# Seven half products for eight in part of layer 1, with conversions in parts and later maxima

## The chip, the cores and the metric

The kernel runs on one core of a Trainium2 chip. TensorE multiplies matrices from SBUF into the accumulator memory PSUM; VectorE, ScalarE and GpSimd work elementwise; the SyncE queue issues most of the transfers. The metric is the device time of one execution in microseconds (us), as the median over runs.

## The reference

Three stages follow one another. Attention gives 1792 tokens of 768 features. Layer 1 makes the largest of three products, and layer 2 projects it. A routed expert layer with two further products ends the program. Layer 1, where the change lies, is this:

```python
def _moe_ref(x, w1, w2, w3, w_out):
    h = np.maximum(np.maximum(x @ w1, x @ w2), x @ w3)   # 1792 x 768, weights 768 x 768
    return (h @ w_out).astype(np.float32)
```

The weights come as 64-bit floats. The kernel turns them into 32-bit ones with integer operations on the two halves of each number.

## The kernel before, in words

Every product is made with 32-bit operands split in two, a rounded part R and the rest L, as three matmuls: R by R, R by L, L by R. In layer 1 the weight is the stationary operand, 128 rows of a feature block at a time, and the tokens stream past it. The 1792 tokens lie as a piece of 1024 and a piece of 768, and the 768 output features are six blocks. `project` (L489) makes one piece of one block of one weight: 6 contraction blocks by 3 matmuls by 2 halves, so 36 matmuls of 512 columns for the piece of 1024, and 36 of 384 columns for the piece of 768. The loop at L529 to L532 goes over block, piece and weight. The first weight of a piece is copied out of PSUM by ScalarE (L503); the second and third are joined by VectorE as a maximum with what lies in SBUF (L505). The result `hT` stays in SBUF: four blocks in `hA` and two in `hB`. PSUM gives these products two buffers in turn (`ps_a`, L160), so a piece must be evacuated before the piece after next begins.

TensorE, ScalarE, VectorE and SyncE run in the order in which the program is written (`manual_schedule`); each is a strict queue, and semaphores make an instruction wait for the others. Layer 1's weights are 18 chunks of 768 x 256 words; w_out gives another 6 of the same size. SyncE loads them into two `stage` buffers (`load_chunk`, L217). VectorE converts one in six operations (`cv_ops`, L166), then ScalarE rounds it and VectorE takes the rest (`split`, L183, with the engines' lines L188 and L189) into one of four slots of `w_ring`. This work and the 48 products that fold the gate matrix into w_out (`gate_op`, L479) lie in two lists, `bg` and `bg2`. `background` (L243) takes operations off them behind each piece until a budget of estimated time is spent. The first four chunks are converted during attention, whose last evacuations are L370 and L371 (`evac_X`).

At the end of layer 1 `split_a` and `split_h` split the first operands of layer 2, which reads the tokens in tiles of 128 (`pass_a`, L566). The expert layer already has products of 384 columns in a scheme with seven products in place of eight (`mm2_prod`, L919); its matmuls have the line L928.

## Time and profile before

| | us |
|---|---|
| median of 3 runs (735.32 to 735.49) | 735.34 |
| the profiled execution itself | 731.45 |
| its span | 729.6 |
| TensorE busy in the span | 721.0 (99%) |
| VectorE busy | 486.5 (67%) |
| ScalarE busy | 263.2 (36%) |
| GpSimd busy | 77.0 (11%) |

The span covers the instructions, and 1.85 us of the profiled execution lie around it. A busy time is the time in which the engine had at least one instruction in work. Matmuls overlap one another in the records, so one matmul's own duration is longer than its share of the stream. The chain of waits is followed back from the last instruction, and its shares say what the span consists of.

### The profile page before, as it was taken

Reading aid. Unit: us, or ns where it says so; the run is one execution under the profiler, and the core shown is the slowest. Engines: PE = TensorE matmul, PEld = TensorE weight load, DVE = VectorE, ACT = ScalarE, POOL = GpSimd, SP = SyncE. Lnnn points to the kernel's source line nnn. Section 1 sums busy time; section 2 is a strip of 40 time slices with the busy share of each in tenths; the row PEclk is TensorE's granted clock in tenths of the full one; section 3 lists DMA queues with packets and bytes.
Section 4 is the critical chain, followed back from the end, with each engine's and each line's share of the span. In section 5 each row is a group of like instructions: output and inputs, shape, how many; then the busy total and the mean of one; then the engine's idle time right before and its main releaser. Section 6 shows DMA issues by size and latency. Waiting matters only on the chain.

```text
span 729.6 us, 10665 instructions
## 1 busy us (share of the span) xinstructions
PE 721.0 (99%) x4164; PEld 613.9 (84%) x4164; DVE 486.5 (67%) x845; ACT 263.2 (36%) x410; POOL 77.0 (11%) x96
## 2 busy tenths in 40 slices
PE   8999999999999999999999999999999999999996
PEld 5455545799898988989899988998998899999996
DVE  4677885666877879873125657146895698689363
ACT  5665566000011010100123533243661474375352
POOL 3000000000000000000001004453025005101101
PEclk9999999999999999999999999999999999999999
DMA  8856761141332321310000113668154025515101
GB/s 204 214 158 167 195 185 54 44 130 54 124 129 91 95 94 44 108 44 1 0 1 22 66 53 126 191 190 308 57 190 158 0 75 174 199 53 193 51 2 63
DMA packets 42330, 78.58 MB, mean 108 GB/s; under 512 B 6201, under 2 KB 28794, under 8 KB 42276
## 3 DMA queue, kind: packets, MB, share of 16 engines
q1 hardware_dynamic: 38420, 66.10, 30.0%
q0 software_dynamic: 3776, 11.63, 4.6%
q8 instruction: 35, 0.57, 0.3%
q14 instruction: 19, 0.16, 0.1%
q10 hardware_dynamic: 80, 0.11, 0.1%
HBM read 69.79 MB, written 11.58 MB: 112 GB/s over the span
## 4 chain that ended last, share of the span: by engine, by line
PE 98%; DMA 0%; SPq 0%; issue 0%; DVE 0%; POOL 0%; POOLq 0%; ACT 0%; ACTq 0%
PE acc L499 36%; PE hacc L900 16%; PE oacc L928 12%; PE X L344 8%; PE s L318 7%; PE acc_b L563 5%; PE acc_a L563 4%; PE oacc L916 3%; PE acc_c L563 3%; PE X L352 2%; PE xT L788 1%; PE s L334 1%; DMA u<-in_qk_dram 0%; SPq L269 0%; PE wgp L360 0%
## 5 line engine op out<-in xcount | busy, mean ns | idle before, releaser
L499 PE MATMUL acc<-xR,w_ring 128*128 128x512 f32 (+1 forms) x864 | 208.3, 362 | 0.0
L499 PEld LDWEIGHTS acc<-xR,w_ring 128*128 128x128 f32 x864 | 157.6, 188 | 17.6 <-issue 0.7
L900 PE MATMUL hacc<-xh,wo_ck 128*128 128x512 f32 (+3 forms) x600 | 120.6, 361 | 0.0
L900 PEld LDWEIGHTS hacc<-xh,wo_ck 128*128 128x128 f32 x600 | 107.1, 188 | 12.1 <-DVE xo L948 0.3
L499 PE MATMUL acc<-xLa,w_ring 128*128 128x512 f32 (+1 forms) x360 | 101.3, 362 | 0.0
L301 ACT ACTIVATE at<-s,nlns 128x896 f32<-128x896 f32 x84 | 77.9, 1007 | 44.4 <-PE s L318 43.0
L928 PE MATMUL oacc<-wo_ck,hx 128*128 128x384 f32 x504 | 90.3, 336 | 0.0
L928 PEld LDWEIGHTS oacc<-wo_ck,hx 128*128 128x128 f32 x504 | 87.2, 188 | 0.2
L189 DVE TENSOR_TENSOR wo_ck<-raw,wo_ck 128x512 fp32r<-128x512 f32 (+1 forms) x87 | 68.4, 807 | 24.6 <-ACT wo_ck L188 24.5
L499 PEld LDWEIGHTS acc<-xLa,w_ring 128*128 128x128 f32 x360 | 66.3, 188 | 7.1
L188 ACT ACTIVATE wo_ck<-raw 128x512 fp32r<-128x512 f32 (+1 forms) x87 | 59.6, 723 | 18.6 <-DVE raw L823 7.6
L318 PEld LDWEIGHTS s<-kq 64*128 64x128 f32 x432 | 37.9, 185 | 21.3 <-issue 15.5
L318 PE MATMUL s<-kq 64*128 64x448 f32 x432 | 50.9, 376 | 0.8 <-ACT kq L287 0.8
L503 ACT ACTIVATE hA<-acc 128x1024 f32<-128x1024 f32 (+1 forms) x8 | 7.4, 922 | 118.3 <-PE acc L499 118.3
L480 DVE SCALAR_TENSOR_TENSOR gk<-wof,gk 128x768 f32<-128x768 f32 x48 | 45.9, 957 | 1.4
L997 POOL MEMSET xo<- 128x544 f32 x5 | 2.6, 550 | 410.6 <-PE acc_a L563 382.1
L775 POOL DMA_INDIRECT xg<-x2d,idx x30 | 36.5, 1218 | 74.1 <-PE xT L788 43.8
L344 PE MATMUL X<-at,u 128*64 128x448 f32 x192 | 37.8, 543 | 0.0
L370 DVE CAST xR<-X 128x448 fp32r<-128x448 f32 x24 | 14.9, 619 | 31.9 <-PE X L352 31.9
L505 DVE TENSOR_TENSOR hB<-hB,acc 128x1024 f32<-128x1024 f32 (+1 forms) x8 | 8.7, 1088 | 39.5 <-PE acc L499 39.4
L188 ACT ACTIVATE w_ring<-cv 128x768 fp32r<-128x768 f32 x14 | 11.8, 842 | 54.7 <-PE acc L499 54.7
L505 DVE TENSOR_TENSOR hA<-hA,acc 128x1024 f32<-128x1024 f32 (+1 forms) x16 | 17.4, 1087 | 20.3 <-PE acc L499 19.9
(260 smaller groups left out, 885.2 us busy)
## 6 DMA issues: line engine op xcount, KB each, us to landing
stage<-in_moe_w_dram SPq DMA_DIRECT2D x18, 768.0 KB, 4.5
raw<-in_moe_w_dram SPq DMA_DIRECT2D x12, 1024.0 KB, 5.7
u<-in_qk_dram SPq DMA_DIRECT2D x46, 224.0 KB, 4.8
raw<-in_moe_w_dram SPq DMA_DIRECT2D x12, 768.0 KB, 4.8
stage<-in_moe_w_out_dram SPq DMA_DIRECT2D x6, 768.0 KB
x2d<-xo SPq DMA_DIRECT2D x28, 128.0 KB, 1.7
gk<-wgT SPq DMA_DIRECT2D x8, 384.0 KB, 5.4
rawb<-in_moe_w_dram SPq DMA_DIRECT2D x4, 768.0 KB, 4.6
```

The lines of the kernel that those rows point to most:

```text
L188: nc.scalar.activation(out=r(dR), in_=src, func=ACTF.Copy)
L189: nc.vector.tensor_tensor(out=r(dL), in0=src, in1=dR, op=ALU.subtract)
L301: nc.scalar.activation(out=dst, in_=s[:, :, 0:S], func=ACTF.Sigmoid, scale=qscale, bias=nlns)
L318: nc.tensor.matmul(s[g][:, h, 0:S], r(kt[p, a, 0, 128 * g:128 * (g + 1)]), r(kt[p, x, 1]), start=(n == 0), stop=(n == 2))
L344: nc.tensor.matmul(X_t[u][64 * h:64 * h + 64, 0:S], vt[:, 2 * g + h], at[:, 2 * g + h], start=(g == 0), stop=False)
L480: nc.vector.scalar_tensor_tensor(out=junk, in0=wof[kb], scalar=1.0, in1=wgb[e % 2], op0=ALU.mult, op1=ALU.mult, accum_out=gw[:, kb, e:e + 1])
L499: nc.tensor.matmul(acc[:, c, 0:cw], r(m[:, a, kk, :]), r(x[kk][:, c0 + cw * c:c0 + cw * (c + 1)]), start=(kk == 0 and n == 0), stop=(kk == ...
L505: nc.vector.tensor_tensor(out=dst, in0=dst, in1=acc[:, :, 0:cw], op=ALU.max)
L563: nc.tensor.matmul(acc, r(hs[:, a, kk, :]), r(w(kk, b)), start=(kk == 0 and n == 0), stop=(kk == KB - 1 and n == 2))
L775: d = nc.gpsimd.indirect_dma_start(out=xg[s][:, XC[c][0]:XC[c][1]], out_offset=None, in_=x2d[c], in_offset=bass.IndirectOffsetOnAxis(ap=ix ...
L900: st["mm"] = nc.tensor.matmul(acc[:, f, t0:t1], r(w[a][:, k, 128 * f:128 * (f + 1)]), r(x[:, 2 * c + k, t0:t1]), start=(t0 == 0 and c == 0 ...
L928: nc.tensor.matmul(o[:, s, 0:HC], r(hz[k][:, x, 2 * c + f, 128 * s:128 * (s + 1)]), r(w[a][:, f]), start=(first and c == 0 and f == 0 and ...
```

## The change

Layer 1's work becomes nine jobs: a pair of feature blocks (256 features) with one of the three weights. Jobs 0 to 4 are made as before, except that the piece of 768 tokens comes first and the order is pair, weight, piece. In jobs 5 to 8 the piece of 768 tokens is made by the Winograd form of Strassen's scheme: the weight pair is a 2 x 2 arrangement of quarters (two feature blocks by two halves of the contraction), the tokens another (two halves of the contraction by two times 384 tokens), and seven half products of 9 matmuls of 384 columns take the place of eight (`s_block`). For that the token operands T1, T2 and T4 are summed and split during job 0 (`t_prep`), T3 in job 4 in the place of an operand that is no longer needed (`t3_prep`), and for each job four sums of weight quarters are made (`s_sums`) and split (`s_split`). The products go to three PSUM banks, two of which are read between two accumulations; VectorE adds the parts and takes the maximum.

A conversion is now one ScalarE copy with a scale and four VectorE operations, and its parts are written between the reads of the products (`hook`). From chunk 16 on there is one stage buffer, and the next load is issued when a conversion has ended. In jobs 5 to 8 the maxima of the piece of 1024 come one piece later (`held`). T4, T1 and T2 lie where `hA` was, so the blocks of the first two pairs are written to DRAM (`spill`) and read back into `hA` in four loads in the last job. The tokens are numbered anew in layer 2 (`tok`), with the piece of 768 first. At the end of attention one further chunk is loaded, and two conversions are begun.

```diff
+    def conv_start(load=True):
+        k = nk[0]
+        nk[0] += 1
+        if k < NC1 and load:
+            load_chunk()
+        v = cv1 if k >= NC1 or k % 2 == 0 else cv2
+        st = stage[k % 2 if k < NC1 else 0]
+        hf = st.bitcast(F32).rearrange("p (n two) -> p n two", two=2)[:, :, 1]
+        nc.scalar.activation(out=v, in_=hf, func=ACTF.Copy, scale=E64_SC)
+        return k, v, st
...
+    def conv_mid(c):
+        v = c[1]
+        ve = nc.vector
+        ve.tensor_scalar(out=v, in0=v, scalar1=-E64_TOP, scalar2=E64_TOP, op0=ALU.max, op1=ALU.min)
+        ve.tensor_scalar(out=v.bitcast(I32), in0=v.bitcast(I32), scalar1=3, scalar2=None, op0=ALU.logical_shift_left)
+    def conv_fin(c, dsts):
+        k, v, st = c
+        st = st.rearrange("p (n two) -> p n two", two=2)
+        lo, hi = st[:, :, 0], st[:, :, 1]
+        ve = nc.vector
+        ve.scalar_tensor_tensor(out=v.bitcast(U32), in0=lo.bitcast(U32), scalar=29, in1=v.bitcast(U32),
+                                op0=ALU.logical_shift_right, op1=ALU.bitwise_or)
+        for d, c0, c1 in dsts or [(v, 0, DM)]:
+            ve.scalar_tensor_tensor(out=d.bitcast(U32), in0=hi[:, c0:c1].bitcast(U32), scalar=0x80000000,
+                                    in1=v[:, c0:c1].bitcast(U32), op0=ALU.bitwise_and, op1=ALU.bitwise_or)
+        if k >= NC1:
+            load_chunk()
...
+    NJOB, FJ = 3 * (KB // 2), 5
...
+    chunks = [wch(j, f) for j in range(2) for f in range(2)] + och(0, 1, 2, 3, 4)
+    chunks += [wch(2, 0)] + och(5) + [wch(2, 1)] + [wch(j, f) for j in range(3, FJ) for f in range(2)]
+    NC1 = len(chunks)
+    assert NC1 % 2 == 0
+    chunks += [wch(j, f) for j in range(FJ, NJOB) for f in range(2)]
+    ring_no = {wch(j, f)[1:]: 2 * (j % 2) + f for j in range(FJ) for f in range(2)}
...
-                background(2.5, stop=(1, 0))
+                background(2.5, stop=(1, 1))
+            if j == NU // 2 - 1:
+                background(99, stop=(1, 1))
+                load_chunk()
             emit_av(A)
             emit_av(B)
-        background(99, stop=(1, 0))
+            if j == NU // 2 - 1:
+                c0 = conv_start(False)
+                early = [c0, conv_start(False)]
+                for c in early:
+                    conv_mid(c)
...
+        SW = (NT - HALF) // 2
+        K2 = KB // 2
+        NQ = K2 * SW
+        S0_, S1_ = slice(HALF, HALF + SW), slice(HALF + SW, NT)
+        tT = hold("H1", "tT", 3, 2, K2, SW)
...
+        def t_prep():
+            tt = hold("K1", "tt", 2, K2, SW)
+            tA, tB = tt[:, 0], tt[:, 1]
+            whole = lambda a: [(slice(0, K2), a)]
+            ops = minus_plus(tA, (xpart(0, 0, S1_)[0][1], xpart(0, 0, S0_)), [(SUB, xpart(1, 0, S0_)), (ADD, xpart(1, 0, S1_))])
+            ops.append(lambda: split(tT[:, 0, 0], tT[:, 0, 1], tA))
+            ops += minus_plus(tB, (xpart(0, 1, S1_)[0][1], whole(tA)), [(ADD, xpart(1, 1, S1_))])
+            ops.append(lambda: split(tT[:, 1, 0], tT[:, 1, 1], tB))
+            ops += minus_plus(tA, (xpart(0, 1, S0_)[0][1], whole(tB)), [(ADD, xpart(1, 1, S0_))])
+            ops.append(lambda: split(tT[:, 2, 0], tT[:, 2, 1], tA))
+            return ops
...
+        def t3_prep():
+            t = cut(sm_[0], 0, K2, SW)
+            for op in minus_plus(t, (xpart(0, 1, S1_)[0][1], xpart(0, 0, S1_)), [(SUB, xpart(1, 0, S1_)), (ADD, xpart(1, 1, S1_))]):
+                op()
+            split(xR_[:, 0:K2, S1_], xLa[:, 0:K2, S1_], t)
...
+        raw_a = [cut(us[i], 2 * DM, QW) for i in range(2)]
+        raw_b = [cut(cv2, QW * i, QW) for i in range(2)]
+        DST = ([(raw_a[i], QW * i, QW * (i + 1)) for i in range(2)], [(cv2, 0, 2 * QW)])
+        def part(i):
+            return cut(sm_[0], QW * i, QW)
+        def s_sums():
+            ve_ = nc.vector.tensor_tensor
+            ve_(out=part(0), in0=raw_b[0], in1=raw_b[1], op=ALU.add)
+            ve_(out=part(1), in0=part(0), in1=raw_a[0], op=ALU.subtract)
+            ve_(out=part(2), in0=raw_a[0], in1=raw_b[0], op=ALU.subtract)
+            ve_(out=part(3), in0=raw_a[1], in1=part(1), op=ALU.subtract)
...
+        def s_split(i):
+            m = sw_[i]
+            split(flat(m[:, 0]), flat(m[:, 1]), cut(sm_[0], 2 * QW * i, 2 * QW))
+        def split_aw(f):
+            if f:
+                split(flat(aw[1][:, 0]), flat(aw[1][:, 1]), cv2)
+                return
+            for k, src in enumerate(raw_a):
+                split(ksl(aw[0], 0, k), ksl(aw[0], 1, k), src)
...
+        def prod(a, b, g, first):
+            a, b = aop(a), bop(b)
+            for kk in range(K2):
+                for n, (i, x) in enumerate(((0, 0), (0, 1), (1, 0))):
+                    nc.tensor.matmul(g[:, 0:SW], r(a(i, kk)), r(b(x, kk)), start=(first and kk == 0 and n == 0),
+                                     stop=(kk == K2 - 1 and n == 2), skip_group_check=not first)
...
+        def s_block(hp, wi, hook):
+            g0, g1 = (ps(f"x{i}", [128, 512], f"g{i}") for i in range(2))
+            g2 = ps("t", [128, 2, 512], "g2")[:, 0]
+            t1, t2, t3, t4 = (part(i) for i in range(4))
+            c = slice(0, SW)
+            ve_ = nc.vector.tensor_tensor
+            def fin(u, g, dst):
+                d = dst if wi == 0 else t4
+                ve_(out=d, in0=u, in1=g[:, c], op=ALU.add)
+                if wi:
+                    ve_(out=dst, in0=dst, in1=t4, op=ALU.max)
+            prod("A11", "B11", g0, True)
+            nc.scalar.activation(out=t1, in_=g0[:, c], func=ACTF.Copy)
+            hook(0)
+            prod("S2", "T2", g1, True)
+            ve_(out=t2, in0=t1, in1=g1[:, c], op=ALU.add)
+            hook(1)
+            prod("A12", "B21", g0, False)
+            take(g0[:, c], hp[:, 0, S0_], wi)
+            hook(2)
+            prod("S1", "T1", g2, True)
+            hook(3)
+            prod("S3", "T3", g1, False)
+            ve_(out=t3, in0=t1, in1=g1[:, c], op=ALU.add)
+            fin(t3, g2, hp[:, 1, S1_])
+            hook(4)
+            g3 = ps("x0", [128, 512], "g3")
+            prod("A22", "T4", g3, True)
+            fin(t3, g3, hp[:, 1, S0_])
+            hook(5)
+            prod("S4", "B22", g2, False)
+            fin(t2, g2, hp[:, 0, S1_])
+            hook(6)
...
+        def spill(p, hp, f, c):
+            nc.sync.dma_start(out=hd[128 * (2 * p + f):128 * (2 * p + f + 1), c], in_=hp[:, f, c])
...
+        tok = list(range(HALF // 128, TT)) + list(range(HALF // 128))
...
-        for fb in range(KB):
-            for half in range(2):
-                for wi in range(3):
-                    project(fb, half, wi)
...
+        plan = {(0, 0): "E T T", (0, 1): "o2 T T", (0, 2): "o3 T T T", (0, 3): "o4 T T T", (1, 0): "w2a", (1, 1): "o5",
+                (1, 2): "w2b"}
+        for j in range(3, FJ):
+            plan.update({(j - 1, 0): f"w{j}a", (j - 1, 2): f"w{j}b"})
+        plan.update({(FJ - 1, 0): "ca", (FJ - 1, 1): "cb", (FJ - 1, 2): "T3", (FJ - 1, 3): "S cn"})
...
+        held = []
+        for j, (p, wi) in enumerate(jobs):
+            if wi == 0:
+                hp = hold("H2", ("h01", "h23", "hB")[p], 2, NT)
+            end = j == NJOB - 1
+            if j < FJ:
+                for n, (c, f) in enumerate(((B1_, 0), (B1_, 1), (B0_, 0), (B0_, 1))):
+                    acc = plain(w_ring[ring_no[2 * p + f, wi]], c.start, c.stop - c.start)
                     step[0] += 1
-                    background(6.6 if half == 0 else 4.8)
-                    if fb == KB - 1 and half == 1:
-                        assert not bg and not bg2
-                        for i in ((0,), (1, 2), ())[wi]:
+                    do_tasks(j, n, 0.0 if wi == 0 else (0.95, 0.95, 1.2, 1.2)[n])
+                    take(acc, hp[:, f, c], wi)
+                    if wi == 2 and p < K2 - 1:
+                        spill(p, hp, f, c)
+                continue
+            split_aw(1)
+            if j == FJ:
+                s_split(1)
+            cb = []
+            def hook(i):
+                step[0] += 1
+                if end:
+                    if i == 4:
+                        background(2.1)
+                elif i == 0:
+                    cb.append(conv_start())
+                elif i == 2:
+                    conv_mid(cb[0])
+                elif i == 4:
+                    conv_fin(cb[0], DST[1])
+            s_block(hp, wi, hook)
+            if wi == 2 and p < K2 - 1:
+                for f in range(2):
+                    spill(p, hp, f, B1_)
+            if end:
+                while bg or bg2:
+                    step[0] += 1
+                    background(9.9)
+                hA = hold("H1", "hA", 4, NT)
+                for c in (S0_, S1_, slice(0, HALF // 2), slice(HALF // 2, HALF)):
+                    nc.sync.dma_start(out=hA[:, :, c], in_=hd.rearrange("(k p) n -> p k n", p=128)[:, :, c])
+                hB = hp
+            for f in range(2):
+                acc = plain(aw[f], 0, HALF)
+                step[0] += 1
+                last = wi == 2
+                if f == 0:
+                    if end:
+                        take(*held.pop())
+                        for i in range(3):
                             split_a(i)
-                        if wi < 2:
-                            hs1[wi] = hs_view(w_ring_[1][:, 0] if wi == 0 else hold("K1", "hs_k", 2 * DM))
-                            split_h(wi, hs1[wi])
+                    else:
+                        s_sums()
+                        for i in range(2):
+                            s_split(i)
+                    if held:
+                        take(*held.pop())
+                    if not end:
+                        background(1.0)
+                    held.append((acc, hp[:, 0, B0_], wi))
+                    continue
+                if end:
+                    take(*held.pop())
+                    for i in range(2):
+                        hs1[i] = hs_view(w_ring_[0][:, 0] if i == 0 else hold("K1", "hs_k", 2 * DM))
+                        split_h(i, hs1[i])
+                else:
+                    ca = conv_start() if j < NJOB - 2 else None
+                    split_aw(0)
+                    if ca:
+                        conv_end(ca, DST[0])
+                    take(*held.pop())
+                    if last:
+                        spill(p, hp, 0, B0_)
+                    background(1.0 if ca else 4.3)
+                if last:
+                    take(acc, hp[:, 1, B0_], wi)
+                    if not end:
+                        spill(p, hp, 1, B0_)
```

## Rows read from the trace of the kernel before

**Rows 1.** The page, chain of work that ended last: by engine, by line

```profile
PE 98%; DMA 0%; SPq 0%; issue 0%; DVE 0%; POOL 0%; POOLq 0%; ACT 0%; ACTq 0%
PE acc L499 36%; PE hacc L900 16%; PE oacc L928 12%; PE X L344 8%; PE s L318 7%; PE acc_b L563 5%; PE acc_a L563 4%; PE oacc L916 3%; PE acc_c L563 3%; PE X L352 2%; PE xT L788 1%; PE s L334 1%; DMA u<-in_qk_dram 0%; SPq L269 0%; PE wgp L360 0%
```

**Rows 2.** Chain of waits in order of time: start us, length us, what

```profile
131.74 259.79 PE acc L499 x1296
391.53 30.54 PE acc_a L563 x252
...
517.12 16.67 PE oacc L928 x96
...
534.66 4.17 PE oacc L928 x24
```

**Rows 3.** Stretches, layer 1 and its end: us, busy by engine, clock, DMA

```profile
131.70:391.50 259.80, 259.80 (x1302) 234.37 (x1299) 173.20 (x285) 25.41 (x36) 0.00 (x0) 1.00 0.21 67
333.80:391.50 57.70, 57.70 (x302) 53.45 (x301) 15.17 (x23) 7.77 (x15) 0.00 (x0) 1.00 0.00 1
```

**Rows 4.** Groups by shape, VectorE: busy us, mean ns, idle before

```profile
L480 DVE SCALAR_TENSOR_TENSOR gk<-wof,gk 128x768 f32<-128x768 f32 x48 | 45.9, 957 | 1.4
...
L176 DVE SCALAR_TENSOR_TENSOR cv<-stage,cv 128x768 uint32<-128x768 uint32 x24 | 23.0, 958 | 0.8
...
L948 DVE SCALAR_TENSOR_TENSOR xo<-oacc,gcol,xo 128x384 f32<-128x384 f32 x24 | 13.9, 612 | 0.0
...
L173 DVE TENSOR_SCALAR cv<-cv 128x768 f32<-128x768 f32 x24 | 13.5, 561 | 0.8
...
L172 DVE TENSOR_SCALAR cv<-stage 128x768 int32<-128x768 int32 x24 | 13.4, 559 | 0.6
...
L505 DVE TENSOR_TENSOR hA<-hA,acc 128x1024 f32<-128x1024 f32 x8 | 9.8, 1219 | 5.2 <-PE acc L499 5.2
...
L505 DVE TENSOR_TENSOR hA<-hA,acc 128x768 f32<-128x768 f32 x8 | 7.6, 955 | 15.0 <-PE acc L499 14.6
...
L189 DVE TENSOR_TENSOR hs_p<-hB,hs_p 128x256 fp32r<-128x256 f32 x7 | 2.9, 421 | 0.0
```

**Rows 5.** The same view, TensorE's weight load and ScalarE

```profile
L928 PEld LDWEIGHTS oacc<-wo_ck,hx 128*128 128x128 f32 x504 | 87.2, 188 | 0.2
...
L188 ACT ACTIVATE w_ring<-cv 128x768 fp32r<-128x768 f32 x14 | 11.8, 842 | 54.7 <-PE acc L499 54.7
...
L503 ACT ACTIVATE hA<-acc 128x1024 f32<-128x1024 f32 x4 | 4.1, 1030 | 34.3 <-PE acc L499 34.3
...
L943 ACT ACTIVATE xo<-oacc,gcol 128x384 f32<-128x384 f32 x6 | 3.5, 584 | 0.0
...
L188 ACT ACTIVATE hs_p<-hB 128x256 fp32r<-128x256 f32 x7 | 2.8, 406 | 0.0
```

**Rows 6.** DMA issues by line: count, KB each, median us to landing

```profile
stage<-in_moe_w_dram SPq DMA_DIRECT2D x18, 768.0 KB, 4.5
raw<-in_moe_w_dram SPq DMA_DIRECT2D x12, 1024.0 KB, 5.7
```

**Rows 7.** VectorE and ScalarE in order of time, start of layer 1

```profile
125.23 0.62 DVE L371 TENSOR_TENSOR xLa<-X,xR 128x448 fp32r<-128x448 f32 x1
131.77 0.62 DVE L370 CAST xR<-X 128x448 fp32r<-128x448 f32 x1 [5.92 <-PE X L352]
...
133.62 0.62 DVE L371 TENSOR_TENSOR xLb<-X,xR 128x448 fp32r<-128x448 f32 x1
...
135.81 1.33 DVE L459 SCALAR_TENSOR_TENSOR bias_t<-midf,mb,bias_t 128x14 f32<-128x14 f32 x8
137.05 0.57 DVE L172 TENSOR_SCALAR cv<-stage 128x768 int32<-128x768 int32 x1
...
140.22 1.03 ACT L503 ACTIVATE hA<-acc 128x1024 f32<-128x1024 f32 x1 [12.28 <-PE acc L499]
```

**Rows 8.** ScalarE in order of time, end of attention

```profile
121.32 6.63 ACT L301 ACTIVATE at<-s,nlns 128x896 f32<-128x896 f32 x7 [3.78 <-PE s L318]
```

More of the change, by code (lines that the diff above doesn't have):

```diff
@@ L126, in attn_moe_kernel @@
     exd = dram.tile([1, 16], I32, name="exd")
+    hd = dram.tile([128 * (KB - 2), NT], F32, name="hd")
     wgT = dram.tile([E, DM], F32, name="wgT")
@@ L222, in load_chunk @@
             src, n = chunk_src(a, b) if kind == "w" else (woi[a * 128:(a + 1) * 128, :].rearrange("p (a c) -> p a c", a=1), 1)
-            nc.sync.dma_start(out=stage[i % 2].rearrange("p (a c) -> p a c", a=n), in_=src)
+            nc.sync.dma_start(out=stage[i % 2 if i < NC1 else 0].rearrange("p (a c) -> p a c", a=n), in_=src)
     bg = deque()
-    for i, (kind, a, b) in enumerate(chunks):
+    for i, (kind, a, b) in enumerate(chunks[:4]):
         bg.append((load_chunk, 0.0, None))
-        ops = cv_ops(i, (lambda: cv1) if kind == "w" else (lambda a=a: wof[a]))
-        bg.extend((op, cost, None) for op, cost in ops)
-        if kind == "w":
-            m = w_ring[ring_no[a, b]]
-            old = [c for c in ring_no if ring_no[c] == ring_no[a, b] and c < (a, b)]
-            first = len(ring_no) and (a, b) <= (1, 0)
-            bg.append((lambda m=m, c=(a, b), first=first: (split(flat(m[:, 0]), flat(m[:, 1]), cv1, first), ready.add(c)),
-                       US_2 + US_1 * first, old[-1] if old else None))
+        bg.extend((op, cost, None) for op, cost in cv_ops(i, lambda: cv1))
+        m = w_ring[ring_no[a, b]]
+        bg.append((lambda m=m, c=(a, b): (split(flat(m[:, 0]), flat(m[:, 1]), cv1, True), ready.add(c)), US_2 + US_1, None))
     bg2 = deque()
@@ L241, in attn_moe_kernel, with background @@
     wof = []
-    def background(us, stop=None, late=2):
-        while us > 0 and (bg or bg2):
+    def background(us, stop=None, late=2, least=0.0):
+        while us > least and (bg or bg2):
             if stop is not None and stop in ready:
@@ L249, in background @@
                 op, cost, _ = bg.popleft()
[L250 removed]
+            elif bg2 and step[0] >= bg2[0][2]:
                 op, cost, _ = bg2.popleft()
@@ L479, in gate_op @@
         def gate_op(e, kb):
-            nc.vector.scalar_tensor_tensor(out=junk, in0=wof[kb], scalar=1.0, in1=wgb[e % 2], op0=ALU.mult,
+            nc.vector.scalar_tensor_tensor(out=junk[0], in0=wof[kb], scalar=1.0, in1=wgb[e % 2], op0=ALU.mult,
                                            op1=ALU.mult, accum_out=gw[:, kb, e:e + 1])
@@ L487, in attn_moe_kernel, with xpart @@
                 bg2.extend((lambda e=e - 1, kb=kb: gate_op(e, kb), US_SUM, 1000 + e - 1) for kb in range(KB))
-        def project(fb, half, wi):
-            while (fb, wi) not in ready:
-                background(0.1, late=0)
-            m = w_ring[ring_no[fb, wi]]
+        def xpart(x, k, c):
+            if x == 0:
+                return [(slice(0, K2), xR_[:, K2 * k:K2 * (k + 1), c])]
+            if k == 0:
+                return [(slice(0, K2), xLa[:, 0:K2, c])]
+            return [(slice(0, K2 - 1), xLa[:, K2:KB - 1, c]), (slice(K2 - 1, K2), xLb[:, :, c])]
@@ new lines, in minus_plus, with step_ @@
+        def minus_plus(d, first, rest):
+            def step_(a, b, op):
+                for sl, ap in b:
+                    nc.vector.tensor_tensor(out=d[:, sl], in0=a[:, sl], in1=ap, op=op)
+            ops = [lambda: step_(*first, ALU.subtract)]
+            ops += [lambda p=p, op=op: step_(d, p, op) for op, p in rest]
+            return ops
+        US_T = 1.35
+        ADD, SUB = ALU.add, ALU.subtract
+        def t_prep():
[8 more added lines that the diff above has]
+            ops.append(lambda: split(tT[:, 2, 0], tT[:, 2, 1], tA))
+            return ops
@@ L500, in project, with take @@
                                          start=(kk == 0 and n == 0), stop=(kk == KB - 1 and n == 2))
-            dst = hT[fb][:, c0:c0 + 2 * cw].rearrange("p (c s) -> p c s", c=2)
+            return acc[:, :, 0:cw]
+        def take(acc, dst, wi):
+            if len(acc.shape) == 3:
+                dst = dst.rearrange("p (c s) -> p c s", c=2)
             if wi == 0:
-                nc.scalar.activation(out=dst, in_=acc[:, :, 0:cw], func=ACTF.Copy)
+                nc.scalar.activation(out=dst, in_=acc, func=ACTF.Copy)
@@ L1024, in end_b @@
         def end_b(p, c=None):
-            rows = slice(128 * toks[p], 128 * (toks[p] + 1))
+            rows = slice(128 * tok[toks[p]], 128 * (tok[toks[p]] + 1))
             a, b = out_b(p, c)
@@ L1036, in put_gate @@
             b = out_b(p, None if p < P0 else 1)[1]
-            nc.vector.tensor_copy(out=b[:, DM - 512:DM - 511], in_=gate[:, toks[p]:toks[p] + 1])
+            nc.vector.tensor_copy(out=b[:, DM - 512:DM - 511], in_=gate[:, tok[toks[p]]:tok[toks[p]] + 1])
         pass_b(0)
```

106 lines of the change are left out of this document (81 added, 25 removed).

## The prediction

> **What bounds the kernel now.** I read the page's chain of waits first: 98% of the span is TensorE, and layer 1's matmul line L499 has 36% by itself [rows 1]. The reader is to see that no other engine and no transfer holds more than a fraction of a per cent. The chain in order of time then shows how tight that is: layer 1 is one piece of 259.79 us with 1296 matmuls [rows 2], and TensorE is busy for all of it at the full clock (2.4 GHz), while VectorE is busy for 173.2 of 259.8 us, and in the last two ninths for only 15.2 of 57.7 [rows 3]. So a matmul taken out of layer 1 comes out of the time, as long as VectorE and ScalarE, which get more work, do not make TensorE wait.
>
> **What one matmul costs.** The expert layer has streams of 384 columns in the same three-matmul manner, in which the weight changes: 24 take 4.17 us, 96 take 16.67 [rows 2]. That is 0.174 us each. It fits layer 1: 259.79 / 648 = 0.401 us for one matmul of 512 and one of 384, which leaves 0.227 for 512. A piece of 768 tokens (36 matmuls of 384) is 6.26 us, a piece of 1024 is 8.16.
>
> **The gain.** In four jobs 63 matmuls of 384 stand for 72: 4 x 9 x 0.174 = 6.26 us less. A block of seven half products lasts 10.97 us where two pieces lasted 12.53, and a job 27.3 us. Everything else of layer 1 on TensorE is the same count in another order.
>
> The page "TensorE: Matmul & The Clock Gate" of the Trainium skill gives, in its section on the back-to-back issue gap, N/2.4 + 2.5 ns for a warm matmul of N columns. By that 384 columns are 162.5 ns and the gain would be 5.85 us, an estimate from the page; the trace's 0.174 decides here.
>
> **What the other engines pay.** VectorE's rows lie on a line: 256 words 0.421, 768 words 0.957 [rows 4], so 1.047 ns a word, 0.56 us for 384 and 1.36 for 1152 (estimates). The only row with 384 words from PSUM, a form with a scalar, has 0.612; I take 0.56 and keep 0.42 and 0.61 as ends. ScalarE by its rows has 0.84 for 768, 0.52 for 384 and 1.17 for 1152; from PSUM 0.58 [rows 5].
> - A conversion was four operations like L172 and L173 (0.56) and two like L176 (0.958): 4.16. Now two and two: 3.04. For 20 chunks VectorE saves 22.4 us. The ScalarE copy that comes in for it reads every second word, which ScalarE does nowhere in the trace. VectorE's L172 does so at the price of L173, which does not. I take 0.84, with 0.58 and twice 0.84 as ends.
> - T1, T2, T4: ten operations, eight of 1152 words (three are the splits' subtractions) and two cut into 768 and 384, 13.9 us in job 0. T3 5.6 in job 4.
> - Four times four weight sums of 0.56 and two split subtractions of 0.958: 16.6.
> - Each block reads its products with nine operations of 0.56 (five in the job that only stores), where two maxima of 0.955 were: 12 more over the four.
>
> The sum is 173 - 22 + 14 + 6 + 17 + 12, some 200 us in 253.5: VectorE remains below TensorE. So the cost lies in single waits, and I walk through those.
>
> **Start of layer 1.** The piece with tokens 1024 to 1791 now comes first, and it reads the columns that the last evacuations write (131.77 to 134.24 [rows 7]). It needs them from the fifth of six contraction blocks on, 131.74 + 4/6 x 6.26 = 135.9. 1.7 us remain, so 0. The two early conversions want ScalarE after its last sigmoid at 127.95 [rows 8] and VectorE between 125.85 and 131.77, where it idles 5.92 us: two copies, then four operations of 0.56, done by about 131. If the cover were gone, at most their 2.3 us would come late, 0.6 of which would reach TensorE.
>
> **Jobs 0 to 4.** VectorE gets free at 137.05 [rows 7]; the two conversions' ends (3.8), T work (13.9) and three conversions (9.1) end at 164, 3.4 us into job 1. There 23.0 us of work (three conversions, two split subtractions, eight gate products of 0.957 [rows 4], four maxima) meet 28.9, and it catches up. TensorE wants no new weight before job 2. Nothing is lost here. The stores to DRAM lie behind a maximum on SyncE, ahead of no load that is due.
>
> **Into job 5 (the one place where I see a wait).** VectorE has T3, the sums, a split and two conversions in job 4, and each conversion's load is issued only when the one before it has ended. Following the queue from job 4's start: first conversion ends at 5.5 (ScalarE still stores job 3's last piece), the second one's chunk lands 4.5 us later [rows 6], it ends at 14.3; T3 and its split 16.3 to 23.2; sums and split to 27.6; the third conversion to 30.9, a maximum to 32.1. Job 5 began at 28.87. Its S3 is ready at +5.2 (wanted at +6.3). The next chunk, issued at +2.0, lands at +6.5; ScalarE's copy ends at +7.4 and VectorE's two operations at +8.7. They stand ahead of the sum t3, which could have begun at +8.2 (product five ends at 7.84, and an evacuation begins 0.32 after the last matmul, as L503 does at 140.22 [rows 7]). t3 and the add that frees g2 end at +9.85. TensorE wants g2 at +9.41: 0.5 us lost. With the ends (copy 1.68, two adds of 0.61) it is 1.4; with 0.58 and 0.42 it is 0.
>
> **Jobs 6 to 8.** The chunk lands at about +2 and the copy is done in time. t3 and the add end at 8.17 + 1.16 = 9.33 and the signal takes a little: against 9.41 that is 0 to 0.1 a job; I take 0.1. After the block: the products' reads end at 14.1, sums 16.4, splits 18.4, ScalarE's or VectorE's held maximum at 17.5 to 18.3, which frees the buffer for the piece at 10.97 + 8.16 = 19.13. 0.8 us remain. VectorE's work in a job is 22 us of 27.3. In job 6 ScalarE's first store must wait for the last DRAM store of job 5, issued at about +1.6 and, of 512 KB, landing by +6.1 if it takes what 768 KB take; the product that needs its bank begins at +7.8.
>
> **The end.** The four loads of `hA` (768, 768, 1024, 1024 KB) are issued when T4 has been read, 9.4 us into job 8. The first lands at 14; layer 2's first split wants it at about 21 and TensorE at 27.3. The others may come one behind another: 2 x 4.5 + 2 x 5.7 = 20.4 [rows 6], so at 29.8, which is before the seventh tile. Layer 2 splits its tiles ahead of their products in the order that it had. So 0.
>
> **Sum.** -6.26 + 0.5 + 0.3 = -5.5 us: the profiled execution's 731.45 becomes 726.0, and the median, which stood 3.89 above it, 735.34 becomes 729.9. All that follows layer 1 moves as a whole: its chain is TensorE's too [rows 1].
>
> **The rivals.**
> - *Late reads.* The single stage buffer and VectorE's strict order make each block wait as job 5 does at its bad end: 4 x 1.4 = 5.6 less the 0.8 counted, so 734.7; half of that, 732.3. For it speaks the margin of 0.1 at g2; against it that the chunk comes 4 us earlier in jobs 6 and 7, and that job 8 converts nothing. I place it at 732 to 735.
> - *The loads of hA.* If the first split waited for all four, layer 2 would begin at 29.8 + 1.5 (its copies and subtractions) where TensorE is ready at 27.3: 4.0 lost, 733.9. Against it: L499 reads `xR` from 131.74 on while L370 still writes other columns of that tile [rows 2, 7], so waits go by columns.
> - *The weight load.* A load's own row is 188 ns [rows 5], more than 174. Were 63 of them the bound of a block, it would take 11.84 and the gain would be 4 x 0.7 = 2.8 us: 733.3. The 24 in 4.17 us, with weights that change, speak against it. In the Trainium skill's page named above, the same section says that in a stream both the weight load and the matmul set the spacing; its 131 ns at 512 columns is not what this trace has (227).
> - *VectorE becomes the bound (slower).* Place: jobs 5 to 8. ScalarE copies that VectorE then waits for, two splits of sums (0.84 each), three of quarters (0.52, 0.52, 0.84) and two conversions (0.84), are 5.2 us a job. Exposed in full they lift 22 to 27.2, a job's whole length, and the waits for products (about 1 us each at t2, t3 and the piece's end) come on top: 3 us a job, 12 in all, 741.1. From 1.6 us a job on nothing is gained, from 1.9 it is slower. For it: strict queues, and dependent pairs on two engines everywhere. Against it: most copies have other VectorE work beside them.
>
> **How the numbers follow.** My forecast 0.60 (728.6 to 731.8; its lower end is the whole gain with no wait), late reads 0.16, loads of `hA` 0.07, weight load 0.05, VectorE as the bound 0.10, something unseen near no change 0.02. A measurement of this kernel can tell 0.2% (1.5 us) from none: faster is below 733.87, slower above 736.81. Faster: 0.60 and most of late reads and of the weight load, 0.13 + 0.04, and half of the loads' case, 0.03: 0.80. Slower: 0.10. Same: the rest, 0.10. Range 728.3 to 735.0: it holds all but the slower case and a few hundredths at either end.
>
> **What would show it.** Layer 1's line count falls from 1296 by 36 and its stretch to about 254.3 us; TensorE's gaps there sum to 1 us at most, the largest at the last product of job 5's block; VectorE is busy about 200 us in it; no gap where layer 2 begins. I would be wrong if gaps stood before every last product, at the pieces after a block, or before the first tile of layer 2, or if a block's 63 matmuls took over 11.2 us without a gap.

## The result and the profile after

| | before | after |
|---|---|---|
| median, us | 735.33 (735.26 to 735.49) | 728.61 (728.36 to 729.89, 4 runs) |
| profiled execution, us | 731.45 | 728.45 |
| its span, us | 729.6 | 726.7 |

The ratio is 0.9912, with an interval of 0.9895 to 0.9929: 6.7 us less, where 5.4 were forecast (729.9). The profiled executions lie only 3.0 us apart, and both differences need an explanation.

The page of the new kernel has a second TensorE line in its chain, `g` at L651. These are the half products; it answers to [rows 1].

```profile
PE 97%; DMA 1%; issue 0%; DVE 0%; SPq 0%; POOL 0%; POOLq 0%; DVEq 0%
PE acc L635 29%; PE hacc L1198 16%; PE oacc L1226 12%; PE X L384 8%; PE s L358 6%; PE g L651 6%; PE acc_b L861 5%; PE acc_a L861 4%; PE oacc L1214 3%; PE acc_c L861 3%; PE X L392 2%; PE xT L1086 1%; PE s L374 1%; DMA u<-in_qk_dram 1%; SPq L309 0%
```

The chain in order of time (start us, length us, what) shows layer 1 as five plain jobs in one piece, and then four times a block of 63 matmuls and a piece of 72. Where one line ends the next begins: the chain has no wait of TensorE in layer 1, and layer 2 (`acc_a`) follows without a gap.

```profile
132.27 144.69 PE acc L635 x720
276.96 10.97 PE g L651 x63
287.93 16.36 PE acc L635 x72
304.29 10.96 PE g L651 x63
...
358.94 10.97 PE g L651 x63
369.92 16.36 PE acc L635 x72
386.28 30.52 PE acc_a L861 x252
```

Layer 1 takes 386.28 - 132.27 = 254.01 us, where it took 259.79 [rows 2]: 5.78 less. The windows (us, then busy time of PE, PEld, DVE, ACT, POOL with their instructions, clock, DMA) of layer 1, of job 5 and of job 8 answer to [rows 3]:

```profile
132.27:386.28 254.01, 254.01 (x1262) 228.18 (x1263) 194.38 (x316) 53.89 (x73) 0.00 (x0) 1.00 0.29 98
276.96:304.29 27.33, 27.33 (x136) 24.48 (x136) 21.90 (x35) 5.73 (x9) 0.00 (x0) 1.00 0.35 117
358.94:386.28 27.34, 27.34 (x138) 24.49 (x137) 15.85 (x30) 4.75 (x12) 0.00 (x0) 1.00 0.39 135
```

VectorE is busy for 194.4 us of it and 21.9 of the fullest job's 27.33; the prediction had some 200 and 22. The granted clock reads 1.00 (2.4 GHz) throughout.

The rest of the profiled difference lies elsewhere: layer 1 begins 0.53 us later, and in the passage from layer 2 to the experts the new kernel's profiled execution has two waits marked "issue", that of before none. The chain there:

```profile
454.21 5.87 PE acc_c L861 x49
460.08 0.70 issue
460.79 0.40 PE acc_c L861 x2
461.19 1.05 issue
462.24 14.54 PE acc_c L861 x120
```

0.70 + 1.05 = 1.75 us. So of the profiled difference of 2.9 us in the spans, -5.78 is layer 1, +0.53 the start and +1.75 this passage, and the remaining +0.6 lies in the rest of the passage and behind it. The start is not layer 1's doing: attention's first product (`X`) already begins 0.46 us later, at 12.10 in place of 11.64. For the other difference, 6.7 against 5.8, the experiments show that the passage is long enough; they do not show that it makes it.

### The profile page after: what moved, and what is told of

The parts are those of the page before. It is cut to its first block, busy times and chain, and to the rows that moved or that the text cites. A ratio compares the mean times of both kernels' runs of the same rounds, so it can differ in the third digit from the quotient of the medians.

```text
span 726.7 us, 10735 instructions
## 1 busy us (share of the span) xinstructions
PE 715.9 (99%) x4128; PEld 608.1 (84%) x4128; DVE 509.7 (70%) x880; ACT 293.5 (40%) x449; POOL 76.8 (11%) x96
## 4 chain that ended last, share of the span: by engine, by line
PE 97%; DMA 1%; issue 0%; DVE 0%; SPq 0%; POOL 0%; POOLq 0%; DVEq 0%
PE acc L635 29%; PE hacc L1198 16%; PE oacc L1226 12%; PE X L384 8%; PE s L358 6%; PE g L651 6%; PE acc_b L861 5%; PE acc_a L861 4%; PE oacc L1214 3%; PE acc_c L861 3%; PE X L392 2%; PE xT L1086 1%; PE s L374 1%; DMA u<-in_qk_dram 1%; SPq L309 0%
## 5 line engine op out<-in xcount | busy, mean ns | idle before, releaser
L635 PE MATMUL acc<-xR,w_ring 128*128 128x512 f32 (+1 forms) x672 | 168.1, 370 | 0.0
L635 PEld LDWEIGHTS acc<-xR,w_ring 128*128 128x128 f32 x672 | 123.5, 188 | 17.6 <-issue 0.7
L635 PE MATMUL acc<-xLa,w_ring 128*128 128x512 f32 (+1 forms) x280 | 81.0, 370 | 0.0
L635 PEld LDWEIGHTS acc<-xLa,w_ring 128*128 128x128 f32 x280 | 51.9, 188 | 7.2
L228 ACT ACTIVATE w_ring<-cv 128x768 fp32r<-128x768 f32 x10 | 8.5, 847 | 70.5 <-DVE cv L213 48.5
L384 PEld LDWEIGHTS X<-at,u 128*64 128x64 f32 x192 | 13.1, 137 | 21.0 <-issue 17.0
L651 PE MATMUL g<-xR,w_ring 128*128 128x384 f32 x96 | 27.1, 336 | 0.0
L1271 POOL DMA_INDIRECT out_dram<-xo,idx x15 | 16.1, 1071 | 96.1 <-DVE xo L1246 49.4
```

What stands on the lines that cost most here:

```text
L228: nc.scalar.activation(out=r(dR), in_=src, func=ACTF.Copy)
L384: nc.tensor.matmul(X_t[u][64 * h:64 * h + 64, 0:S], vt[:, 2 * g + h], at[:, 2 * g + h], start=(g == 0), stop=False)
L635: nc.tensor.matmul(acc[:, c, 0:cw], r(m[:, a, kk, :]), r(x[kk][:, c0 + cw * c:c0 + cw * (c + 1)]), start=(kk == 0 and n == 0), stop=(kk == ...
L651: nc.tensor.matmul(g[:, 0:SW], r(a(i, kk)), r(b(x, kk)), start=(first and kk == 0 and n == 0), stop=(kk == K2 - 1 and n == 2), skip_group_ ...
```

## The experiments

Theory A: layer 1's time is its matmuls' time, the change is worth the 5.8 us of the matmuls left out, and the rest of any difference is the passage. The rivals were that the new order itself, the conversions in parts or the later maxima cost or bring time by themselves. Runs of one batch share a chip and the runs of the kernel before: 735.02 us in the first, 731.67 in the second, 735.44 in the third, 732.34 in the fourth.

**The kernel before, profiled again.**

> The kernel before, unchanged, to learn where its two levels come from (a profiled execution of 731.45 us, a median of 735.3 us). Theory A: the two are executions with and without a wait of some 4 us that lies outside layer 1; then the spans of its runs fall on two levels, layer 1 is 259.8 us in each, and the new kernel's whole gain of 6.7 us is 5.8 us of layer 1 and 0.9 us of a wait that this execution happens to have. Theory B: all its executions outside the one profiled have something slower in layer 1 that the change removed; then a profile at 735 us has a layer 1 of about 263 us. Expected by A: median 735.3, spans at 733.5 or 729.6.

735.09 us (734.29 to 736.71); the profiled execution took 734.75, 3.3 more than the first. Layer 1 is the same to the hundredth. The passage, from the first `acc_c` to the expert layer's first matmul (`hacc`), is not: 485.38 - 459.68 = 25.70 us, where the first execution had 22.45.

```profile
131.93 259.79 PE acc L499 x1296
...
466.65 0.84 issue
...
474.83 1.30 issue
...
479.08 4.52 DMA xg<-x2d,idx
...
485.38 0.12 PE hacc L900
```

So 3.25 of the 3.89 us between profiled execution and median, which the prediction carried over as a constant, can be this passage. TensorE waits 0.84 us in it for nothing that the profile shows ("issue") and 1.62 us for the gather of the expert layer's tokens; the second "issue", 1.30 us, is a wait of ScalarE ahead of that gather. The expectation's lower level, a span of 729.6, came in none of the 12 executions here (732.5 to 735.0).

**The new kernel, profiled again on another chip.**

> The new kernel, unchanged, with as many runs on this chip as the kernel before. Theory A: layer 1 is 254.0 us in its profile again, and the ratio to before is that of 5.8 us of 735, 0.992, give or take the 1 us by which the passage from layer 2 to the experts differs between executions (22.4 to 26.1 us in the five profiles so far). So 728.5 to 729.8. Rival: the first measured 6.7 us hold a second gain outside layer 1; then the passage is shorter here than in most runs of before and the time is below 728.5.

726.52 us (726.14 to 728.26), ratio 0.9933 with 0.9919 to 0.9946: 5.15 us less than before there. Layer 1 took 254.02. This time the passage has no wait:

```profile
454.68 20.51 PE acc_c L861 x171
...
477.14 0.12 PE hacc L1198
```

477.14 - 454.68 = 22.46 us. Either kernel can have the short or the long passage. In the profiles of the first and the third batch, where the kernel before stands at 735.0 and 735.4, the passage takes 23.8 to 26.1 us, whatever the kernel; in those of the second and the fourth, where it stands at 731.7 and 732.3, it takes 22.4 to 22.7. So its length goes with the batch, that is with the chip or the time; which of the two is open. My figures for the absolute time were off by that level. Layer 1's 5.8 us are firm; how much of the passage adds to them or hides them differs.

**An eighth product in each block.** The whole new order, with 9 matmuls more a block, which nothing reads.

```diff
-            g2 = ps("t", [128, 2, 512], "g2")[:, 0]
+            gt = ps("t", [128, 2, 512], "g2")
+            g2 = gt[:, 0]
...
+            prod("A22", "B22", gt[:, 1], True)
             prod("S4", "B22", g2, False)
```

> The new kernel with an eighth half product of 9 matmuls in each of the four blocks, written to the free half of a PSUM pair and read by nothing; all other work and its order stay. Theory A (the time of layer 1 is the count of its matmuls): each block grows by 9 x 0.174 = 1.57 us, layer 1 from 254.0 to 260.3, the time from 728.6 to 734.9. Rival (the order, the cheaper conversions or the early piece give a good part of the gain): the time stays below 732. Second rival (VectorE sets the blocks' length): the time stays below 731, since the added product fills waits.

735.94 us (734.68 to 736.93), ratio 1.001 with 0.9999 to 1.002. Layer 1 took 392.52 - 132.31 = 260.21 us, its blocks 12.52:

```profile
277.00 12.52 PE g L651 x72
...
392.52 30.52 PE acc_a L863 x252
```

The gain in layer 1 is the matmuls left out and nothing else: with eight products the new order is as fast as the old one, to 0.4 us.

**The conversion in one piece, ahead of the second product's read.**

```diff
                 elif i == 0:
-                    cb.append(conv_start())
-                elif i == 2:
-                    conv_mid(cb[0])
-                elif i == 4:
-                    conv_fin(cb[0], DST[1])
+                    conv_end(conv_start(), DST[1])
```

> The second conversion of each of the jobs 5 to 7 is written whole behind the first product in place of three parts between the reads. Theory A (VectorE's strict queue holds the product reads behind a conversion whose chunk has not landed): in job 5 ScalarE's copy ended 5.6 us into the block, four operations of 3.0 us and the read of the second product follow at 9.2, and the fifth product, which wants that read at 6.3, begins 3.0 us late; jobs 6 and 7 lose 0.3 to 0.5 each. Time 728.6 + 3.8 = 732.4, with a gap ahead of the fifth product of job 5. Rival (VectorE has room, the parts don't matter): within 0.5 us of 728.6.

734.07 us (732.85 to 734.77), ratio 0.998 with 0.9969 to 0.9992. Layer 1 took 259.95 us, 5.94 more than with the parts: the whole gain is gone. Job 5's block took 15.65 us in place of 10.97, jobs 6 and 7 11.6 each. The chain in job 5:

```profile
276.77 4.28 DMA stage<-in_moe_w_dram
...
281.13 0.91 ACT cv L195
...
284.25 0.96 DVE cv L213
...
285.20 0.48 DVE sm L671
...
285.72 6.30 PE g L651 x27
```

The chunk lands, ScalarE and VectorE convert it, and only then does VectorE read the product that frees the bank. Two more views, TensorE's order of time and the window of those 27 matmuls, show that this is not all:

```profile
285.72 0.69 PE L651 MATMUL g<-xR,w_ring 128*128 128x384 f32 x1 [3.07 <-DVE sm L671]
```

```profile
285.70:292.02 6.32, 6.30 (x28) 6.30 (x29) 3.21 (x6) 0.00 (x0) 0.00 (x0) 0.77 0.38 127
```

The wait is 3.07 us, but 27 matmuls at 0.174 are 4.70, not 6.30. The granted clock in that window is 0.77: after the wait TensorE ran at the lower level (1.2 GHz) for a while. 3.07 + 1.60 is the 4.68 that the block lost. Not all of the 1.60 is the clock. In jobs 6 and 7 the wait at the same place is short (0.32 us in job 6), the clock behind it reads 1.00, and the 27 matmuls still take 0.30 more than 4.70:

```profile
314.98 5.00 PE g L651 x27
```

That leaves some 1.30 for the lower clock, an estimate from these two jobs. The expectation, at 3.0 us for this job, had the wait right and lacked the clock. The edit puts a conversion in one piece and puts it early; a whole conversion at a later place was not tried.

**Each maximum behind its own product.** `held` is taken out; the rest is the new kernel.

```diff
+                    take(acc, hp[:, 0, B0_], wi)
                     if end:
-                        take(*held.pop())
...
-                    if held:
-                        take(*held.pop())
...
-                    held.append((acc, hp[:, 0, B0_], wi))
...
-                    take(*held.pop())
...
-                if last:
-                    take(acc, hp[:, 1, B0_], wi)
-                    if not end:
-                        spill(p, hp, 1, B0_)
-                else:
-                    held.append((acc, hp[:, 1, B0_], wi))
+                take(acc, hp[:, 1, B0_], wi)
+                if last and not end:
+                    spill(p, hp, 1, B0_)
```

> The maxima of the piece of 1024 in jobs 5 to 8 are written right behind their product, ahead of the sums and splits, in place of one piece later. Theory A (there is room in the piece that follows): the sums start 20.7 us into the job, splits end at 25, the copy for the next job's first weight at 27, with 27.3 as the limit: 0 to 0.7 us a job, time 728.6 to 731. Rival (the late maxima are what keeps TensorE fed): the next block begins 2 to 3 us late in each of three jobs, time 735 to 738.

733.72 us (732.33 to 735.43), ratio 0.9981 with 0.9968 to 0.9994. Layer 1 took 259.33 us, 5.32 more, and all of it at one place that neither theory had named, in job 6's block; jobs 7 and 8 lost nothing.

```profile
307.01 1.15 DVE h L645
...
308.18 6.66 DMA hd<-h
...
314.94 0.50 ACT hB L643
...
315.48 4.91 PE g L651 x18
```

The maximum now waits for its product, VectorE is late with everything behind it, and the store of job 5's last quarter to DRAM is issued at 308.18. SyncE's queue had just issued the load of the next chunk (306.23), another store of 512 KB (306.67) and a load of 384 KB (307.25); in the new kernel these three are issued 4 us and more ahead of that store (300.05 to 301.47, the store at 305.58). It takes 6.66 us. ScalarE's first store into the buffer `hB` waits for it, and the product that needs the bank waits for ScalarE. TensorE's row there reads a wait of 3.50 us; the 18 matmuls behind it took 4.91 in place of 3.13, at a granted clock of 0.65. 3.50 + 1.78 is 5.28 of the 5.32. In the new kernel the same ScalarE store stands at 309.03 and waits for its product only.

**Five and six weight pairs by seven products.** FJ is the number of plain jobs; the gate products, which fill VectorE's gaps, are spread anew, since more of them have to find room later.

```diff
-    NJOB, FJ = 3 * (KB // 2), 5
+    NJOB, FJ = 3 * (KB // 2), 4
...
+                elif i == 3:
+                    background(2.2 if wi == 0 else 1.1)
...
-                        background(1.0)
+                        background(2.2 if wi == 0 else 1.1)
...
-                    background(1.0 if ca else 4.3)
+                    background((4.6 if wi == 0 else 3.4) if ca else 6.7)
```

> Five weight pairs by seven products in place of four (jobs 4 to 8), with the gate products spread over the new blocks: one or two ahead of the third read, more behind the maxima. Theory A (layer 1 is its matmul count as long as VectorE has room): one more block, 1.57 us less: layer 1 252.4, time 1.6 below the new kernel. VectorE's busy time in layer 1 rises from 194 to about 202 of 252. Rival (the gate products ahead of the third read delay the bank that the seventh product wants): up to 0.5 us a block, no gain.

> Six weight pairs by seven products (jobs 3 to 8), the gate products spread in the same manner. Theory A: two more blocks, 3.1 us less: layer 1 250.9, time 3.1 below the new kernel, if the gate products are through by the last job. VectorE then has about 210 of 251 us. Rival (VectorE becomes the bound at the end): one to five gate products are left over when the last block ends and stand ahead of the maximum that frees the last piece's buffer, which has 1.6 us of room: up to 3 us lost there, no gain over four pairs.

Five pairs (FJ = 4): 725.06 us (724.66 to 725.23), 1.46 less than the new kernel on the same chip; layer 1 took 252.67, 1.35 less, where one more product left out is 1.57; its first block took 11.06 and one piece of 72 took 16.45, 0.09 more than the others each. Six pairs (FJ = 3) with the same spreading: 725.12 us, and layer 1 took 253.36, since the first block (job 3) needed 13.4 us. TensorE's rows there:

```profile
227.41 1.83 PE L651 MATMUL g<-tT,w_ring 128*128 128x384 f32 x9 [0.47 <-ACT h L643]
...
230.58 0.45 PE L651 MATMUL g<-xR,w_ring 128*128 128x384 f32 x1 [1.34 <-DVE h L663]
```

The granted clock reads 1.00 behind both waits, whose rows make 1.81 of the 2.4 us. The later blocks ran in 10.97. The loss is at the beginning, where I had looked for it at the end: the chain runs over VectorE's queue and its loads from 132 us on (T1 to T4, the conversions and the gate products). The chunk for this block lands 6.4 us into it (225.5; in the new kernel's first block 4.7); ScalarE's store ahead of the first wait follows the copy of that chunk and a store to DRAM (0.46 us), and a conversion's middle part and two gate products stand ahead of the reads that free the bank of the second.

**Six pairs, VectorE's load ahead of job 3 lighter.**

```diff
-                background(max(left, 0.1), least=1.0 if j else 0.0)
+                background(min(max(left, 0.1), 3.0), least=1.0 if j else 0.0)
...
                 elif i == 3:
-                    background(2.2 if wi == 0 else 1.1)
+                    if j > FJ:
+                        background(1.1)
```

> Six weight pairs by seven products, with VectorE's load ahead of job 3 made lighter: at most three units (3.0 us) of gate products behind a piece in jobs 0 to 2, none inside job 3's block, one in each later block; what is left over falls into job 8, where VectorE idles about 10 us. Theory (the first block's loss comes from VectorE being late before it): job 3's block runs in 11.0 to 11.5 instead of 13.4, layer 1 takes 251.0 to 251.6, 1.0 to 1.5 us less than with five pairs in the same batch. Rival (the single stage buffer's load, which can't be issued before the conversion ahead of it, is late in any case): job 3's block still loses 1.5 us or more, and the total stays within 0.5 us of five pairs.

> Five pairs by seven products once more, as the neighbour of the run above on the same chip: layer 1 252.7 as before, 1.3 to 1.5 us below four pairs; the total 6.5 to 8.5 us below the kernel before, by how long the passage from layer 2 to the experts takes in either kernel on this chip.

732.45 us (731.13 to 733.91), ratio 0.9956 with 0.9943 to 0.9969, slower than five pairs in the same batch (726.43, ratio to before 0.9875 with 0.9861 to 0.989; its layer 1 took 252.67). The theory about job 3 held: its block took 10.97. But the edit did two things, VectorE's load before job 3 and the two gate products inside its block, and no run separates them. The gate products that had been put off all fell into job 8:

```profile
379.43 0.96 DVE L531 SCALAR_TENSOR_TENSOR gk<-wof,gk 128x768 f32<-128x768 f32 x1
...
380.32 1.22 DVE L645 TENSOR_TENSOR hB<-hB,acc 128x1024 f32<-128x1024 f32 x1
```

```profile
381.68 1.04 PE L635 MATMUL acc<-xR,w_ring 128*128 128x512 f32 x2 [4.78 <-DVE hB L645]
```

```profile
381.68:391.70 10.02, 10.02 (x38) 8.12 (x39) 4.92 (x11) 0.62 (x2) 0.00 (x0) 0.83 0.00 0
```

The first row is the last of nine gate products in a row ahead of the held maximum (L645), which frees a PSUM buffer. TensorE waited 4.78 us, and the piece behind it took 10.02 us in place of 8.17, at a granted clock of 0.83 in the third view: 1.85 us on top. Without both, layer 1's 257.66 would have been 251.0.

**The left-over gate products of job 8 put elsewhere.**

```diff
                 if end:
-                    if i == 4:
-                        background(2.1)
+                    if i in (0, 1, 2, 4):
+                        background(1.0 if i < 2 else 2.1)
...
-                while bg or bg2:
-                    step[0] += 1
-                    background(9.9)
...
                     if end:
                         take(*held.pop())
+                        while bg or bg2:
+                            step[0] += 1
+                            background(9.9)
                         for i in range(3):
                             split_a(i)
```

> The run before with the leftover gate products of job 8 put elsewhere: one behind each of the first two half products, up to three behind the third, two behind the fifth, and what is left only behind the first held maximum. Theory (in the run before, 9 gate products in a row held up the maximum that frees a PSUM buffer, 4.8 us, and TensorE came back at half clock, 1.85 us more): job 8 takes 27.3 instead of 34.0, layer 1 251.0 to 251.5, 1.2 to 1.7 below five pairs in the same batch; the total 0.5 to 2 us below five pairs. Rival (VectorE's work in job 8 is too much wherever it stands): a gap of 2 us or more remains in job 8 or before layer 2's first tile, and the total does not beat five pairs.

> Five pairs by seven products as the neighbour on the same chip: layer 1 252.7 again.

723.50 us (723.16 to 723.98), ratio 0.9882 with 0.9865 to 0.99; five pairs on the same chip took 724.83 (724.62 to 724.92). Layer 1 took 383.33 - 132.32 = 251.01 us, six blocks at 10.95 to 10.97 without a wait in the chain; five pairs there 384.63 - 131.90 = 252.73. This is the fastest version of the study, 8.8 us below the kernel before. The first and last lines of its chain in layer 1, and its window:

```profile
132.32 86.95 PE acc L635 x432
219.27 10.96 PE g L651 x63
...
356.00 10.97 PE g L651 x63
...
383.33 30.52 PE acc_a L864 x252
```

```profile
132.32:383.33 251.01, 251.01 (x1245) 225.03 (x1245) 206.94 (x344) 57.34 (x80) 0.00 (x0) 1.00 0.29 99
```

## Why the prediction was right, and where its terms were off

**The gain, 6.26 us.** The mechanism is shown: the run with eight products gave all of it back. Its size in layer 1 was 5.78. A block took 10.97, as forecast; its neighbours took a little more than reckoned: a piece of 72 took 16.36 where 16.33 was reckoned (0.13 in four), and the five plain jobs 144.69 where five ninths of [rows 2] are 144.33. That 0.36 does not grow with the plain jobs: three took 86.95 (fj3c) and five 144.69, so one takes 28.87, as before, and 0.34 is lost once, in the first three jobs or where they begin. One row shows a part of it, in job 1:

```profile
173.74 0.30 PEld L635 LDWEIGHTS acc<-xR,w_ring 128*128 128x128 f32 x2 [0.21 <-DVE h L645]
```

The weight load ahead of job 1's third piece waits 0.21 us for a maximum with which VectorE is late. The same wait, 0.21 to 0.26 us, stands at this place in every run of the new order, so "Nothing is lost here" for jobs 0 to 4 was a little off. What the rest is stays open.

**Job 5's wait, 0.5 us: mis-sized, it is 0.** The order of events was right and the queue's lengths were not. VectorE's and ScalarE's rows in job 5:

```profile
277.25 1.21 DVE L645 TENSOR_TENSOR h<-h,acc 128x1024 f32<-128x1024 f32 x1
278.38 0.95 DVE L229 TENSOR_TENSOR w_ring<-cv,w_ring 128x768 fp32r<-128x768 f32 x1
...
284.82 0.55 DVE L679 TENSOR_TENSOR sm<-sm,g 128x384 f32<-128x384 f32 x1 [1.06 <-PE g L651]
285.41 0.55 DVE L663 TENSOR_TENSOR sm<-sm,g 128x384 f32<-128x384 f32 x1
```

```profile
281.67 0.91 ACT L195 ACTIVATE cv<-stage 128x768 f32<-128x768 f32 x1 [2.60 <-DMA stage<-in_moe_w_dram]
```

The chunk is there at 281.67, 4.7 us into the job and not 6.5, so `t3` no longer stands behind the conversion but waits for its product, and the add that frees `g2` ends at 285.96, +9.0 where TensorE wants it at +9.41. The queue of job 4 was 1.7 us shorter than my sum of durations: its last conversion ended at 29.2 us from the job's start, reckoned 30.9. Part of that is that an operation which does not need the one ahead starts before that one ends (278.38 where the first ends at 278.46). The unknown durations were near the values taken: 0.91 for ScalarE's copy of every second word (0.84), 0.55 for an addition from PSUM (0.56).

**Jobs 6 to 8, 0.1 each: mis-sized, it is 0.** The blocks took 10.96 to 10.97. The prediction put 0.32 us between a product's last matmul and its read and so reckoned `t3` at +8.17. It starts at +7.86 in job 5 (284.82 above) and at +7.86 to 7.87 in jobs 6 to 8 (312.15, 339.47, 366.81), where the fifth product ends at +7.84. So the add that frees `g2` ends at +9.0 in all four blocks, in place of 9.33 in three of them, and the margin was 0.4 us, not 0.1.

**Start and end, 0: right.** The last evacuations begin at 132.30 in the new kernel, and TensorE's first piece shows no wait for them. At the end of layer 1, VectorE's and the DMA queue's rows:

```profile
379.29 0.69 DVE L229 TENSOR_TENSOR w_ring<-hA,w_ring 128x512 fp32r<-128x512 f32 x1
...
386.32 1.22 DVE L645 TENSOR_TENSOR hB<-hB,acc 128x1024 f32<-128x1024 f32 x1 [5.07 <-PE acc L635]
```

```profile
368.36 2.36 SPq L801 DMA_DIRECT2D hA<-hd  x4
```

```profile
368.40:379.30 10.90, 10.90 (x51) 9.24 (x50) 10.31 (x22) 3.14 (x8) 0.00 (x0) 1.00 0.93 324
```

The first tile's split begins at 379.29, 10.9 us after the loads were issued and 7 before layer 2. By then 10.9 us at 324 GB/s, 3.53 of the four loads' 3.67 MB, had been moved (last number of the window); from 380 on the queues move nothing. So the four took under 12 us, where the prediction's bound was 20.4.

**The rivals.** The weight load as a bound fell with 63 matmuls, each with its own 188 ns load, in 10.97 us. VectorE as the bound fell even for six blocks: 206.94 of 251.01 us busy and no wait in the chain. Late reads did not happen, but the run with whole conversions shows what late reads cost: 5.94 us, near the 5.6 that I gave this rival at its bad end, but divided otherwise. I had 1.4 in each of four jobs; it was 4.68 in job 5, the lower clock in it, and 0.63 in jobs 6 and 7 each.

**The median, 729.9 against 728.61.** Layer 1 gave 0.3 us more than the forecast's 5.5. The other 0.9 of the measured 6.7 is not layer 1; the passage behind layer 2, 22.4 to 25.7 us in the two executions of the kernel before, is large enough for it. Which passage the unprofiled executions had is not known, and what makes its waits come and go was not tried. That the median came out near the lower end of the forecast's 728.6 to 731.8 is in part luck: layer 1's gain alone would have made it 729.6.

## What to carry to other kernels

Where one engine is busy all the time, work taken out of it comes out of the time one to one, as long as the other queues keep their reads in time. Here that took parts that fit between the reads: the same operations in one piece ahead of a read cost 5.9 us, the whole gain. Price a wait of the matrix engine with what its clock does after it, and look for it at the point where the helper engine has been late the longest, not only where its load is greatest. Work that can be put off needs a place of its own: nine operations left over to the end cost 6.6 us, spread over the idle stretches of the same job they cost nothing.

## What the runs showed of the hardware

- After waits of 3.07, 3.50 and 4.78 us TensorE's granted clock read 0.77, 0.65 and 0.83 in the stretch that followed, and the stretch took 1.60, 1.78 and 1.85 us longer. After waits of up to 1.6 us (0.32 in the run with whole conversions, 1.34 with six pairs, 1.62 in the passage of the kernel before) it read 1.00; behind the 0.32 the stretch still took 0.30 longer. The Trainium skill, "TensorE: Matmul & The Clock Gate", section "HAM oscillation — how this bites in real kernels", says that a long wait between bursts of matmuls sends the engine back to its lower clock, and that the next burst pays for it; the three runs agree.
- A 512 KB store issued within 2 us of a 768 KB load, another 512 KB store and a 384 KB load on the same queue took 6.66 us, where [rows 6] have a median of 4.5 for a 768 KB load. Four loads of 768 to 1024 KB issued together on one queue were through in under 12 us (324 GB/s between 368.40 and 379.30), where the medians of [rows 6] add up to 20.4.
- The same program's passage between two stages took 22.45 us in one execution and 25.70 in another, with waits that the profile marks "issue" and a wait for a gather that the shorter one does not have.
